# Eight instead of six of sixteen masked row block pairs merged by a VectorE copy, the two new ones in the half unit of the value products

## The chip, the core and the metric

The kernel runs on one core of a Trainium2 chip. The metric is the device time of one execution in microseconds (us), as the median of several runs. TensorE (PE in the profile; its weight loads are PEld) does the matmuls, VectorE (DVE) and ScalarE (ACT) read what it leaves in PSUM, GpSimd (POOL) works on SBUF alone, and SyncE (SP) issues nearly all DMAs.

## The reference, cut to what matters

A block with conditioning runs a sliding-window attention and then a token-mixing and a channel MLP on 2048 rows of 576. What the change touches is the attention: 32 heads of 18, and each row sees itself and the 255 rows before it.

```python
scores = jnp.einsum("bhqd,bhkd->bhqk", q, k) * (Dh ** -0.5)
idx = jnp.arange(S)
mask = (idx[:, None] - idx[None, :] >= 0) & (idx[:, None] - idx[None, :] < W)   # W = 256
scores = jnp.where(mask[None, None], scores, -1e9)
p = _softmax(scores, axis=-1)
o = jnp.einsum("bhqk,bhkd->bhqd", p, v)
```

## The kernel before, in words

The kernel has five stages: the projection to q, k and v (function `qkv`), the attention (`attention`, with the output projection and the two norms behind it, `wotile`), the token mixing (`mixing`), and the channel MLP (`mlp`). Each step is a small function, put on a list with a time by `at(t, f)`; the list is sorted by that time and run through, so the order of the instructions on each engine is written by hand. The times are an order only: each engine works through its queue in that order and waits on semaphores for what it needs.

The attention counts in half units, `n` from 0 to 31, each with the scores of two groups (`j` = 0, 1) of two heads for 512 rows; a unit `u` is two half units. Two things happen to the scores, a half unit or two apart:

- *The row maxima.* `mx(n, j, bb)` (lines 515 to 525) takes a pair of row blocks: for each of two blocks of 64 rows, one matmul (L519) gives 128 rows (two heads) by five key blocks of 64 in PSUM tile `mx`. Of the five key blocks the oldest and the newest are cut by the window's edge and by the diagonal. Where a pair isn't merged, a second matmul (L523) adds the mask `Mq` to these two blocks through the identity. `red(n, j, bb)` (lines 527 to 541) then takes the maximum of the 2 x 320 columns on VectorE (L537). In a merged pair there is no mask matmul. Where the late block is cut, the early one isn't, and the other way round, so that VectorE copies by predicate the early block over the masked places of the late one (L534) and takes the maximum of 2 x 256 columns (L535). `merged(n, j, bb)` says which of the sixteen pairs of a unit are merged (8 in each half unit: `j` 0 and 1, `bb` 0 to 3).
- *The exponentials.* Two half units and a little later `xm` computes the scores again with keys in rows (L568, and masks by L570) into two score banks `X` in turn, with the maximum folded in, and `ex` takes the exponential on ScalarE (L585).

The tiles `mx` have two buffers, by the parity of `bb`: the matmuls of a pair wait until the reduction of the pair two before has read its buffer.

In every even half unit from n = 4 on, `av(u)` gives the products of the exponentials with the values: 72 to 104 small matmuls in one go (L607), between the first pair (`mx` 0_0) and the second (0_1). Later in the same half unit their sum is copied (L612, ScalarE), turned by transposes `ot` (L617, two times four), and normalised on VectorE (`onm`: a reciprocal L624 and a product L625, each once for `r` = 0 and 1). From n = 12 to 30 the even half unit also begins one tile of the output projection: transposes `pa` and `pb` (L671, L673) into the same PSUM banks that `ot` had, copies by ScalarE (L678, L679), and the low parts by VectorE (L680, L681); its matmuls (L692) and the norm's statistics come in the odd half unit.

Of the kernel before, what the change touches and what calls it, by code (L numbers as in the profile page):

```python
# [33 lines left out]
class Kern:  # L34
# [418 lines left out]
    def attention(self, t1, t2, TA, HU, LX=2.05):  # L453
# [52 lines left out]
                nc.gpsimd.tensor_scalar(t[:, b0:, r], src[:, b0:], M[:, 2 + r:3 + r], 0.0, op0=ALU.mult, op1=ALU.add)  # L506

        def merged(n, j, bb):
            return (n >= 8 or bb >= 2) and (n % 2, j, bb) in ((0, 0, 0), (1, 0, 0), (1, 0, 1), (1, 0, 3), (1, 1, 0), (1, 1, 3))

        def mx(n, j, bb):
            g = n // 8
            pm = X["pm", n, j, bb] = ps.tile([P, 2, 512], F32, tag=f"m{bb % 2}", name=f"mx{n}_{j}_{bb}")
            Q, K = X["qs", n, j], X["K"][n % 3]
            for s in range(2):
                i = 2 * bb + s
                nb = 5 if g else min(5, i + 1)
                lhs = Q[:, i].rearrange("p r q -> p (r q)")
                nc.tensor.matmul(pm[:, s, 320 - 64 * nb:320], lhs, K[:, j, 64 * (i + 5 - nb):64 * (i + 5)], start=True, stop=merged(n, j, bb))  # L519
                if merged(n, j, bb):  # L520
                    continue
                if nb == 5:
                    nc.tensor.matmul(pm[:, s, 0:320].rearrange("p (a b) -> p a b", b=64)[:, 0::4, :], self.identr, self.Mq, start=False, stop=True)  # L523
                else:
                    nc.tensor.matmul(pm[:, s, 256:320], self.identr, self.Mq[:, 1], start=False, stop=True)

        def red(n, j, bb):
            if ("m", n) not in X:
                X["m", n] = a1([P, 16], F32, tag="m", name=f"m{n}", bufs=2)
            m, pm = X["m", n], X["pm", n, j, bb]  # L530
            c = 8 * j + 2 * bb
            if merged(n, j, bb):
                late = self.Mq[:, 1].bitcast(mybir.dt.int32).unsqueeze(1).to_broadcast([P, 2, 64])
                nc.vector.copy_predicated(pm[:, :, 256:320], late, pm[:, :, 0:64])  # L534
                nc.vector.tensor_reduce(out=m[:, c:c + 2], in_=pm[:, :, 64:320], axis=mybir.AxisListType.X, op=ALU.max, negate=True)  # L535
            elif n >= 8 or bb >= 2:
                nc.vector.tensor_reduce(out=m[:, c:c + 2], in_=pm[:, :, 0:320], axis=mybir.AxisListType.X, op=ALU.max, negate=True)  # L537
            else:
                for s in range(2):
                    w = 64 * (2 * bb + s + 1)  # L540
                    nc.vector.tensor_reduce(out=m[:, c + s:c + s + 1], in_=pm[:, s, 320 - w:320], axis=mybir.AxisListType.X, op=ALU.max, negate=True)
# [860 lines left out]
```

## Time and profile before

| | |
|---|---|
| median of 3 runs | 1775.26 us (1769.92 to 1777.12) |
| the profiled execution | 1768.65 us, span 1766.8 us |
| granted TensorE clock, mean | 0.984 |
| projections and before | up to about 211 us |
| attention, first eight half units | about 211 to 305 us |
| attention, the others | about 305 to 610 us |
| end of the attention, output projection of its last tiles | 610 to 671 us |
| token mixing and MLP | 671 to 1766.8 us |
| TensorE busy from 305 to 610 us | 298.12 of 305.00 us |
| VectorE busy from 305 to 610 us | 221.53 of 305.00 us |

The span is the time from the first to the last instruction of one execution; the device time has a little around it. An engine's busy time counts instructions that overlap once, and matmuls are pipelined: the mean duration of one is longer than the time that it adds to a queue. The chain of waits gives the latter, since it goes from start to start. In the rows, L523 is line 523 of the kernel, the number behind `x` is a count, and an arrow names what ended a wait.

### The profile page before, as it was taken

How to read it: one execution, taken by the hardware profiler on the slowest of the kernel's cores; microseconds unless marked ns; L12 is line 12 of the kernel's file. 1: busy time of each engine (PE TensorE's matmuls, PEld its weight loads, DVE VectorE, ACT ScalarE, POOL GpSimd, SP SyncE). 2: the span in 40 equal slices, each digit the busy share in tenths (PEclk: the TensorE clock that was granted, in tenths of full speed). 3: DMA queues.
4: the chain of work that ended last, by engine and by line, in shares of the span. 5: the costliest groups of instructions: out<-in, count | busy, mean ns of one | idle time of the engine just before them, and what ended most of it. 6: DMA issues, size and time to landing. Idle time of an engine off the chain costs nothing.

```text
span 1766.8 us, 33658 instructions
## 1 busy us (share of the span) xinstructions
PE 1677.2 (95%) x13369; PEld 1530.6 (87%) x13369; DVE 1106.2 (63%) x1887; ACT 704.6 (40%) x1211; POOL 898.2 (51%) x837
## 2 busy tenths in 40 slices
PE   6999998999999989987899999999899999999998
PEld 5888898899999978987688999999788999999997
DVE  6544265677777637665576666666675666666664
ACT  3222134555455454444343334433434333334331
POOL 4222357545546433555665665555635555665550
PEclk9999999999999999999899999999999999999999
DMA  8854554546556266644422112222142221112211
GB/s 259 274 178 167 169 147 131 159 133 192 151 162 172 88 189 208 208 139 154 157 63 61 47 51 63 63 64 63 59 137 60 64 63 57 44 58 63 63 45 54
DMA packets 156501, 206.79 MB, mean 117 GB/s; under 512 B 19316, under 2 KB 87924, under 8 KB 155768
## 3 DMA queue, kind: packets, MB, share of 16 engines
q1 hardware_dynamic: 155768, 203.46, 37.4%
q8 instruction: 106, 1.74, 0.4%
q10 hardware_dynamic: 576, 1.18, 0.2%
q14 instruction: 51, 0.42, 0.1%
HBM read 143.76 MB, written 60.56 MB: 116 GB/s over the span
## 4 chain that ended last, share of the span: by engine, by line
PE 80%; DVE 6%; POOL 4%; DMA 4%; issue 3%; ACT 3%; SPq 1%; POOLq 0%; DVEq 0%; ACTq 0%
PE d L1256 24%; PE qk L331 6%; PE mx L519 4%; PE X L568 4%; PE av L607 4%; PE wo L692 3%; PE v L369 3%; PE X L570 2%; PE pg L916 2%; PE w L965 1%; DVE W L1114 1%; PE ot L617 1%; DMA wmf<-in_w_mod_dram 1%; PE mx L523 1%; DMA wf<-in_B_w_dram 1%
## 5 line engine op out<-in xcount | busy, mean ns | idle before, releaser
L1256 PEld LDWEIGHTS d<-W,G 128*128 128x128 f32 x3456 | 489.4, 189 | 34.7 <-DVE acc L1264 10.1
L1256 PE MATMUL d<-W,G 128*128 128x288 f32 x3456 | 507.7, 297 | 12.2 <-DVE acc L1264 9.0
L1264 DVE TENSOR_TENSOR acc<-d,acc 128x576 f32<-128x576 f32 x288 | 216.8, 754 | 199.6 <-PE d L1256 197.5
L1094 POOL TENSOR_TENSOR wf<-wf 128x384 f32<-128x384 f32 x140 | 147.0, 1070 | 339.7 <-DMA wf<-in_B_w_dram 331.6
L585 ACT ACTIVATE P<-X 128x512 f32<-128x512 f32 (+4 forms) x320 | 178.2, 572 | 112.4 <-PE X L570 110.0
L537 DVE TENSOR_REDUCE m<-mx 128x2 f32<-128x640 f32 x144 | 117.9, 820 | 91.7 <-PE mx L523 91.1
L1233 DVE TENSOR_TENSOR G<-U,G 128x512 fp32r<-128x512 f32 x108 | 92.8, 859 | 99.4 <-ACT G L1226 99.4
L519 PE MATMUL mx<-KD,QS 128*128 128x320 f32 (+4 forms) x512 | 143.5, 340 | 11.0 <-DVE m L537 4.2
L1106 POOL TENSOR_TENSOR W<-wf,W 128x768 fp32r<-128x768 f32 x70 | 152.9, 2206 | 1.2 <-ACT W L1100 1.2
L568 PE MATMUL X<-QD,KS 128*128 128x64 f32 (+2 forms) x704 | 142.8, 295 | 3.0 <-ACT P L585 2.2
L1224 ACT ACTIVATE U<-U 128x512 f32<-128x512 f32 x108 | 68.3, 632 | 178.7 <-DVE U L1209 178.7
L499 POOL TENSOR_SCALAR QS<-QD,rowm 128x512 fp32r<-128x512 f32 x128 | 87.1, 694 | 96.3 <-DMA QD<-qd 41.5
L1224 ACT ACTIVATE C<-C 128x512 f32<-128x512 f32 x36 | 22.8, 632 | 282.5 <-DVE C L1209 282.5
L568 PEld LDWEIGHTS X<-QD,KS 128*128 128x128 f32 x704 | 106.7, 191 | 8.7 <-ACT P L585 4.8
L331 PE MATMUL qk<-hT,Wqk 128*128 128x512 f32 x462 | 109.3, 396 | 1.1 <-DVE qs L345 1.1
L506 POOL TENSOR_SCALAR KS<-KD,rowm 128x768 fp32r<-128x768 f32 (+1 forms) x128 | 108.8, 863 | 0.0
L519 PEld LDWEIGHTS mx<-KD,QS 128*128 128x128 f32 x512 | 93.1, 193 | 16.4 <-issue 7.2
L1120 POOL TENSOR_TENSOR wf<-wf,gb 128x1152 f32<-128x1152 f32 x35 | 103.1, 2945 | 7.2 <-DMA wf<-in_B_w_dram 7.2
L331 PEld LDWEIGHTS qk<-hT,Wqk 128*128 128x128 f32 x462 | 86.4, 188 | 23.4 <-DVE qs L345 1.6
L1135 POOL TENSOR_TENSOR W<-wf,W 128x1152 fp32r<-128x1152 f32 x35 | 96.7, 2763 | 6.9 <-ACT W L1129 6.9
L1100 ACT CAST W<-wf 128x1152 fp32r<-128x1152 f32 x70 | 90.4, 1320 | 20.0 <-DMA wf<-in_B_w_dram 10.5
L570 PE MATMUL X<-Mk,identr 128*128 128x256 f32 (+2 forms) x320 | 95.2, 297 | 0.0
(787 smaller groups left out, 3208.4 us busy)
## 6 DMA issues: line engine op xcount, KB each, us to landing
wf<-in_B_w_dram SPq DMA_DIRECT2D x35, 576.0 KB
wf<-in_B_w_dram SPq DMA_DIRECT2D x140, 128.0 KB
KD<-kd SPq DMA_DIRECT2D x72, 216.0 KB
QD<-qd SPq DMA_DIRECT2D x96, 144.0 KB
wf<-in_B_w_dram SPq DMA_DIRECT2D x140, 64.0 KB
qd<-qs SPq DMA_DIRECT2D x16, 512.0 KB
kd<-qs SPq DMA_DIRECT2D x16, 512.0 KB
vd<-Vst SPq DMA_DIRECT2D x16, 312.0 KB
```

The source lines that it names most:

```text
L331: nc.tensor.matmul(po, W[:, a, fs], H[:, c, :], start=(n == 0), stop=(n == 13))
L506: nc.gpsimd.tensor_scalar(t[:, b0:, r], src[:, b0:], M[:, 2 + r:3 + r], 0.0, op0=ALU.mult, op1=ALU.add)
L519: nc.tensor.matmul(pm[:, s, 320 - 64 * nb:320], lhs, K[:, j, 64 * (i + 5 - nb):64 * (i + 5)], start=True, stop=merged(n, j, bb))
L537: nc.vector.tensor_reduce(out=m[:, c:c + 2], in_=pm[:, :, 0:320], axis=mybir.AxisListType.X, op=ALU.max, negate=True)
L568: nc.tensor.matmul(px[:, c:c + q1 - q0], K[:, b + 4].rearrange("p r k -> p (r k)"), Q[:, j, q0:q1], start=(i == 0), stop=False)
L570: nc.tensor.matmul(o, self.identr, mv, start=False, stop=True)
L585: nc.scalar.activation(p[:, lo:], X["px", n, j, k][:, lo:], AF.Exp, scale=SCALE)
L1094: nc.gpsimd.tensor_tensor(out=WF[:, o], in0=WF[:, a], in1=WF[:, b], op=ALU.subtract)
L1106: eng.tensor_tensor(out=W[:, s0:s1, 3:5, :], in0=WF[:, 1 + s0:1 + s1, 0:2], in1=W[:, s0:s1, 0:2, :].bitcast(F32), op=ALU.subtract)
L1120: nc.gpsimd.tensor_tensor(out=R4, in0=R4, in1=gb.unsqueeze(1).to_broadcast([P, 2, D]), op=ALU.mult)
L1256: nc.tensor.matmul(po, G[:, g, ta, b, ts], W[:, w, b, cs], start=(n == 0), stop=(n == 5))
L1264: nc.vector.tensor_tensor(out=a, in0=po, in1=a, op=ALU.add)
```

## The change

The tuple of pairs that are merged gets two more entries, (0, 0, 1) and (0, 1, 1): the second pair of each `j` in the even half unit.

```diff
         def merged(n, j, bb):
-            return (n >= 8 or bb >= 2) and (n % 2, j, bb) in ((0, 0, 0), (1, 0, 0), (1, 0, 1), (1, 0, 3), (1, 1, 0), (1, 1, 3))
+            return (n >= 8 or bb >= 2) and (n % 2, j, bb) in ((0, 0, 0), (0, 0, 1), (0, 1, 1), (1, 0, 0), (1, 0, 1), (1, 0, 3), (1, 1, 0), (1, 1, 3))
```

On TensorE in an even half unit, just behind the value products, before (the names are those of the tiles, written and read, with their numbers):

```order
 L545 MATMUL mt_6046<-ident,m_5763 16x128
 L519 MATMUL mx_0_1_6062<-KD_1992,QS_0_5884 128x320
 L523 MATMUL mx_0_1_6062<-Mq,identr 128x2x64
 L519 MATMUL mx_0_1_6062<-KD_1992,QS_0_5884 128x320
 L523 MATMUL mx_0_1_6062<-Mq,identr 128x2x64
 L568 MATMUL X_0_1_6073<-QD_1988,KS_0_5839 128x192
```

and in the same place now:

```order
 L545 MATMUL mt_6034<-ident,m_5751 16x128
 L519 MATMUL mx_0_1_6050<-KD_1992,QS_0_5872 128x320 x2
 L568 MATMUL X_0_1_6059<-QD_1988,KS_0_5827 128x192
 L568 MATMUL X_0_1_6059<-QD_1988,KS_0_5827 128x320
 L570 MATMUL X_0_1_6059<-Mk,identr 128x2x128
```

The two mask matmuls are gone, and the score matmuls of `xm` follow the two of `mx` at once; nothing else has moved.

On VectorE in the second part of the same half unit, around the second new pair, before:

```order
 L537 TENSOR_REDUCE m_5935<-mx_1_0_6132 128x2
 L624 RECIPROCAL rc_0_6151<-ot_0_6138 128x16
 L625 TENSOR_TENSOR o_6150<-ot_0_6138,rc_0_6151 128x16x18
 L537 TENSOR_REDUCE m_5935<-mx_1_1_6154 128x2
 L624 RECIPROCAL rc_1_6174<-ot_1_6159 128x16
 L625 TENSOR_TENSOR o_6150<-ot_1_6159,rc_1_6174 128x16x18
 L537 TENSOR_REDUCE m_5935<-mx_1_2_6182 128x2
 L680 TENSOR_TENSOR T_6198<-pa_6191,T_6198 128x512
```

and now:

```order
 L537 TENSOR_REDUCE m_5923<-mx_1_0_6119 128x2
 L624 RECIPROCAL rc_0_6138<-ot_0_6125 128x16
 L625 TENSOR_TENSOR o_6137<-ot_0_6125,rc_0_6138 128x16x18
 L534 COPY_PREDICATED mx_1_1_6141<-Mq,mx_1_1_6141 128x2x64
 L535 TENSOR_REDUCE m_5923<-mx_1_1_6141 128x2
 L624 RECIPROCAL rc_1_6160<-ot_1_6144 128x16
 L625 TENSOR_TENSOR o_6137<-ot_1_6144,rc_1_6160 128x16x18
 L537 TENSOR_REDUCE m_5923<-mx_1_2_6168 128x2
 L680 TENSOR_TENSOR T_6184<-pa_6177,T_6184 128x512
```

A copy stands ahead of the reduction of pair 1_1, between the two normalisations, and that reduction is the narrow one.

## The prediction

> **What bounds the kernel now.** I read the page's first lines, then the costs by shape, then the busy time of the two kinds of half unit that alternate through the attention stage, then the waits, and last the chain of waits and the timeline of one unit. The page first:
>
> ```profile
> span 1766.8 us, 33658 instructions
> PE 1677.2 (95%) x13369; PEld 1530.6 (87%) x13369; DVE 1106.2 (63%) x1887; ACT 704.6 (40%) x1211; POOL 898.2 (51%) x837
> ```
>
> TensorE is busy for 95% of the span and VectorE for 63%, so on the whole the span is TensorE's queue. The sum below is made against this execution: 1768.65 us of device time around a span of 1766.8. It is a quick one; the runs shown have 1775.26 as their median (1769.92 to 1777.12), 6.6 us more, and I carry the difference that I work out over to that median.
>
> The costs by shape of what is removed and added (count, then busy us and mean ns of one):
>
> ```profile
> L523 PE MATMUL mx<-Mq,identr 128*128 128x128 f32 x288 | 64.6, 224 | 0.0
> L537 DVE TENSOR_REDUCE m<-mx 128x2 f32<-128x640 f32 x144 | 117.9, 820 | 91.7 <-PE mx L523 91.1
> L535 DVE TENSOR_REDUCE m<-mx 128x2 f32<-128x512 f32 x80 | 55.3, 692 | 2.8
> L534 DVE COPY_PREDICATED mx<-Mq,mx 128x128 f32<-128x128 int32 x80 | 22.9, 286 | 2.6 <-PE mx L519 2.4
> ```
>
> The 80 copies are the pairs that are merged today, and the 144 wide reductions are the pairs that still get two mask matmuls each (288). All four operations of the change are in the trace already, at the shapes that the change uses.
>
> Busy time by stretch: the first row is a half unit with value products, the second the half unit behind it.
>
> ```profile
> core 0: us, PE busy (x) PEld busy (x) DVE busy (x) ACT busy (x) POOL busy (x), PEclk, DMA share, GB/s
> 477.06:491.42 14.36, 14.21 (x282) 13.07 (x282) 10.23 (x18) 7.54 (x15) 11.39 (x17) 1.00 0.67 203
> 491.42:504.18 12.76, 12.37 (x92) 11.86 (x91) 9.60 (x22) 6.69 (x13) 2.90 (x6) 1.00 0.33 91
> ```
>
> TensorE fills 14.21 of 14.36 us where the change acts, at a granted clock of 1.00; VectorE fills 10.23. The waits of the attention stage (time, times, longest) say the same from the other side:
>
> ```profile
> DVE m L537 <- PE mx L523: 91.1, 99, 5.0
> PE mx L519 <- DVE m L537: 4.2, 12, 1.7
> ```
>
> VectorE waits 91.1 us for the mask matmul; TensorE waits only 4.2 us for a reduction, so VectorE has time to give, but not everywhere.
>
> **The change, part by part.** *How many.* A half unit n merges only where n is at least 8 or bb at least 2. The new entries are (0, 0, 1) and (0, 1, 1), both with bb = 1, so they act in the even half units n = 8 to 30: 12 halves, 24 pairs (the first four units gain none, so that eight of sixteen holds for the last twelve alone). Removed: 48 mask matmuls with their weight loads. Added: 24 copies. Turned from 640 to 512 columns: 24 reductions. No DMA, no tile and no other queue changes.
>
> *What a pair saves on TensorE.* The row of 224 ns is no price, because matmuls overlap. The chain of waits gives the time that each adds (start, us, what): an unmerged pair at the place of the first new one, and two pairs that are merged today.
>
> ```profile
> 482.66 0.15 PE mx L519
> 482.81 0.06 PE mx L523
> 482.87 0.20 PE mx L519
> 483.07 0.06 PE mx L523
> ...
> 496.88 0.29 PE mx L519 x2
> ...
> 497.47 0.41 PE mx L519 x2
> ```
>
> Unmerged 0.15 + 0.06 + 0.20 + 0.06 = 0.47 us, merged 0.29 us with score matmuls behind it: 0.18 us saved. With output-projection matmuls behind it (497.47) it takes 0.41, and 0.06 is saved. The new pairs are followed by score matmuls and by the second transposes of the value products, so I take 0.18: 24 x 0.18 = 4.3 us. The ends are 24 x 0.06 = 1.4 us, and 48 x 0.224 = 10.8 us if the whole row were time of the queue.
>
> [...]
>
> The score matmuls of a pair shrink too, from 0.15 and 0.20 to 0.29 for both; that is why a pair saves more than its two mask matmuls' 0.12.
>
> *What a pair costs on VectorE.* Its timeline over the even half unit, and a merged pair of the next one:
>
> ```profile
> 483.17 0.82 DVE L537 TENSOR_REDUCE m<-mx 128x2 f32<-128x640 f32 x1 [2.37 <-PE mx L523]
> ...
> 487.63 0.46 DVE L625 TENSOR_TENSOR o<-ot,rc 128x288 f32<-128x288 f32 x1
> 488.01 0.82 DVE L537 TENSOR_REDUCE m<-mx 128x2 f32<-128x640 f32 x1
> 488.74 0.25 DVE L624 RECIPROCAL rc<-ot 128x16 f32<-128x16 f32 x1
> 489.02 0.46 DVE L625 TENSOR_TENSOR o<-ot,rc 128x288 f32<-128x288 f32 x1
> 489.77 0.82 DVE L537 TENSOR_REDUCE m<-mx 128x2 f32<-128x640 f32 x1 [0.29 <-PE mx L523]
> 490.82 0.69 DVE L680 TENSOR_TENSOR T<-pa,T 128x512 fp32r<-128x512 f32 x1 [0.23 <-ACT T L678]
> ...
> 497.49 0.28 DVE L534 COPY_PREDICATED mx<-Mq,mx 128x128 f32<-128x128 int32 x1
> 497.81 0.69 DVE L535 TENSOR_REDUCE m<-mx 128x2 f32<-128x512 f32 x1
> 498.41 0.28 DVE L534 COPY_PREDICATED mx<-Mq,mx 128x128 f32<-128x128 int32 x1
> ```
>
> From start to start the wide reduction takes 488.74 - 488.01 = 0.73 us, copy and narrow reduction 498.41 - 497.49 = 0.92: 0.19 more for each pair. The first new pair (483.17) comes after 2.37 us of idling, so its 0.19 us costs nothing as long as the reductions behind it wait for TensorE, as most do by the 99 waits above. The second (488.01) has no idle time in front, as it stands between the two normalisations. By the first pair's saving all up to there slides 0.18 earlier, to 487.83; with 0.92 for the pair the reciprocal starts at 488.75 (before 488.74), the normalisation at 489.03, and VectorE is free at 489.49. The next reduction's matmuls are ready 0.36 earlier, at 489.41: it starts 0.08 late. That is paid from the 0.23 us of idle time in front of the projection's copy L680. So the price on the path is nothing; the cover is this 0.23, and were it gone, 12 x 0.08 = 1.0 us would be late.
>
> *Who else has to keep up.* ScalarE's exponentials set when a score bank is free:
>
> ```profile
> 483.60 0.60 ACT L585 ACTIVATE P<-X 128x512 f32<-128x512 f32 x1 [0.64 <-PE X L570]
> 487.59 0.60 ACT L585 ACTIVATE P<-X 128x512 f32<-128x512 f32 x1 [0.21 <-PE X L570]
> ```
>
> The first exponential behind the first new pair had waited 0.64 us for TensorE, and the one ahead of the second had waited 0.21: ScalarE's work starts from TensorE's and slides with it. The last stretch of the half unit leads from TensorE over ScalarE and VectorE (L680, L681, L537) back to TensorE:
>
> ```profile
> 489.73 0.45 PE pa L671 x4
> 490.18 0.02 issue
> 490.20 0.59 ACT T L678
> ...
> 492.50 0.56 PE mx L519 x2
> ```
>
> It begins with a TensorE transpose (489.73) that comes 0.36 earlier, so its end, the matmul that waits for the last reduction at 492.50, comes 0.36 earlier too.
>
> *The sum.* 12 half units x 2 pairs x (0.18 on TensorE + 0 on VectorE) = 4.3 us, which nothing behind the stage gives back, as the stages that follow start from its last matmul. 1768.65 - 4.3 = 1764.4 for an execution like the profiled one; 1775.26 - 4.3 = 1771.0 for the median, 0.24% less. By over 0.5% (8.9 us) is about what a measurement of this kernel can tell from no change, so I forecast no difference that can be told.
>
> **Rivals.**
>
> *The whole busy time goes.* If the queue shortened by 0.224 us for each removed matmul, 10.8 us, the median would be 1764.5, 0.6% faster. For it: TensorE is the bound and its weight loads go as well. Against it: the chain gives these matmuls 0.06 us each, and a pair 0.18.
>
> *VectorE becomes the bound: slower than before.* The place is the transpose pb, which writes the bank that the second normalisation reads:
>
> ```profile
> 490.00 0.27 PE L673 MATMUL pb<-ident,or 128*128 128x128 f32 x1
> ```
>
> It would come at 489.64, and VectorE has finished at 489.49. If VectorE is over 0.15 us later than I work out, TensorE's whole queue stands there, the saving is eaten, and at worst the extra 0.19 of each of the 24 pairs comes on top: 4.6 us, 1779.9. For it: there is no idle time between 487.63 and 489.02. Against it: 0.29 and 0.23 of idle time follow. To be slower by over 0.5% each of the 12 units would have to lose 0.74 us, more than a whole wide reduction holds VectorE (0.73).
>
> [...]
>
> *Only the first pair counts.* If the three-engine stretch from 489.73 to 492.50 is held by VectorE or ScalarE, the second saving is idle time: 12 x 0.18 = 2.2 us, 1773.1. For it: TensorE does wait there. Against it: the stretch starts from TensorE.
>
> **How the numbers follow.** The forecast has 0.72, only the first pair 0.13, the whole busy time 0.07, VectorE the bound 0.08. With the runs spread over 7.2 us, about 0.05 of the forecast's chance comes out over 0.5% faster, so faster is 0.07 + 0.05 = 0.12; half of VectorE's case is put beyond 0.5%, so slower is 0.04; the same is left 0.84. The range goes from 1764.5 less 1.5 to 1779.9, the ends of the unknown costs: 1763 to 1780. The likeliest case alone, with its ends of 1.4 and 4.3 and half the spread, is 1767 to 1777.
>
> **What would show it.** Mask matmuls L523 240 in place of 288, L537 120, L534 and L535 104 each. In the chain, the pair behind the value products at about 0.29 in place of 0.47. A half unit with value products of 14.0 in place of 14.36 us, the other unchanged at 12.76, and the reduction at 489.77 without idle time in front of it. A row "PE pb" that waits for VectorE, or a wait of TensorE for a reduction much over 4.2 us in sum, would show the VectorE rival, and a unit that is shorter by 0.18 that only the first pair counts. The forecast is wrong if the half units shorten and the end of the program does not.

## The result and the profile after

The changed kernel takes 1762.08 us (median of 4 runs, 1759.46 to 1764.23), the kernel before beside it 1775.9 (1769.92 to 1777.12): a ratio of 0.9946, 95% interval 0.992 to 0.9973, so 9.6 us less, with 4.8 to 14.2 possible. (The two medians, of four runs each, lie 13.8 us apart; that is near the far end of the interval.) Two repeats on other occasions gave 0.9947 (0.9925 to 0.9968) and 0.9949 (0.9926 to 0.9973). The forecast was 0.9976. The gain is real and about twice the 4.3 us of the sum; the question is where the other half is from.

The profiled execution after took 1759.46 us. Its page, and the groups by shape that the change touches:

```profile
span 1757.6 us, 33586 instructions
...
PE 1668.2 (95%) x13321; PEld 1522.8 (87%) x13321; DVE 1108.8 (63%) x1911; ACT 704.3 (40%) x1211; POOL 898.9 (51%) x837
```

```profile
L537 DVE TENSOR_REDUCE m<-mx 128x2 f32<-128x640 f32 x120 | 98.0, 819 | 51.0 <-PE mx L523 50.5
...
L535 DVE TENSOR_REDUCE m<-mx 128x2 f32<-128x512 f32 x104 | 71.9, 691 | 3.6
...
L523 PE MATMUL mx<-Mq,identr 128*128 128x128 f32 x240 | 53.5, 223 | 0.0
...
L534 DVE COPY_PREDICATED mx<-Mq,mx 128x128 f32<-128x128 int32 x104 | 29.9, 287 | 36.6 <-PE mx L519 36.5
```

The counts are those forecast: 48 matmuls and 48 weight loads fewer, 24 copies more. VectorE's 91.1 us of waiting for the mask matmul has become 50.5 + 36.5 us, the latter in front of the copy, which now waits for the score matmul. The waits of the attention stage and the two half units that the prediction showed:

```profile
DVE m L537 <- PE mx L523: 50.5, 75, 2.1
...
DVE mx L534 <- PE mx L519: 36.5, 17, 6.1
...
PE mx L519 <- DVE m L537: 4.0, 12, 1.6
```

```profile
473.40:487.10 13.70, 13.70 (x278) 12.93 (x278) 10.45 (x20) 7.53 (x15) 10.73 (x17) 1.00 0.69 205
487.10:499.87 12.77, 12.39 (x92) 11.89 (x92) 9.61 (x22) 6.70 (x13) 3.55 (x6) 1.00 0.38 100
```

TensorE waits for a reduction as little as before (4.0 us, before 4.2). The half unit with value products went from 14.36 to 13.70 us, the other stayed (12.76, now 12.77). In the chain of waits of that half unit (start, us, what) both new pairs are short, and the stretch over ScalarE and VectorE at its end is what it was:

```profile
478.54 0.21 PE mt L545
478.74 0.29 PE mx L519 x2
...
483.35 0.30 PE mx L519 x2
...
485.42 0.45 PE pa L671 x4
...
488.19 0.57 PE mx L519 x2
```

VectorE's timeline there:

```profile
479.07 0.29 DVE L534 COPY_PREDICATED mx<-Mq,mx 128x128 f32<-128x128 int32 x1 [1.94 <-PE mx L519]
...
483.87 0.28 DVE L534 COPY_PREDICATED mx<-Mq,mx 128x128 f32<-128x128 int32 x1
484.19 0.69 DVE L535 TENSOR_REDUCE m<-mx 128x2 f32<-128x512 f32 x1
484.80 0.25 DVE L624 RECIPROCAL rc<-ot 128x16 f32<-128x16 f32 x1
485.08 0.46 DVE L625 TENSOR_TENSOR o<-ot,rc 128x288 f32<-128x288 f32 x1
485.45 0.82 DVE L537 TENSOR_REDUCE m<-mx 128x2 f32<-128x640 f32 x1
486.51 0.69 DVE L680 TENSOR_TENSOR T<-pa,T 128x512 fp32r<-128x512 f32 x1 [0.23 <-ACT T L678]
```

The first new copy has 1.94 us of idle time ahead of it, the second none, and the reduction at 485.45 starts without idle time and not late: it stands 0.03 us behind the transpose `pa` (485.42), before 0.04 (489.77 and 489.73).

To see where the 9.1 us between the two profiled executions lie, I took the starts of the same TensorE instruction in both (us; *av* is the first value product L607, *mt* L545, *wo* the run of L692 of a group):

```
                                                     before   after   difference
start to the first av                                252.34  249.31     -3.03
first to sixth av (three changed half units)         116.52  117.65     +1.13
sixth av to the last half unit (nine changed)        247.27  242.75     -4.52
last half unit to the last av                         14.19   15.60     +1.41
last av to the first wo behind it (the 21st group)    13.71   10.56     -3.15
21st to 23rd wo                                        9.68    6.90     -2.78
from there to the end                               1113.08 1114.88     +1.80
```

The first row can't be the change, since up to there both kernels issue the same instructions; it is the granted clock (a window of before, then of after, from 220 to 230 us, the clock third from the right):

```profile
220.00:230.00 10.00, 8.83 (x40) 8.05 (x41) 6.25 (x16) 0.25 (x1) 6.06 (x10) 0.67 0.59 170
```

```profile
220.00:230.00 10.00, 9.17 (x60) 8.00 (x60) 8.03 (x21) 0.25 (x1) 6.33 (x10) 1.00 0.72 225
```

The +1.41, -2.78 and +1.80 have such stretches at half clock in them too (3.4 us from 613.6 on and from 794.5 on in after only, 6.8 us from 643.2 on in before only). The second row, whose three changed half units should give -1.1, holds the value products, whose time varies from unit to unit (from 4.74 to 6.21 us, below). What is left is the stage and the 3.15 us from the first of the last value products to the output projection, which no term of the sum names. Of the stage's 4.52, the value products, whose time varies, hold 1.2; the parts of the half units that the pairs are in hold the other 3.3 (nine half units). The timelines there, TensorE's rows and then the first of ScalarE's weight copies L849; before:

```profile
630.32 4.31 PE L607 MATMUL av<-P,V 64*32 64x320 f32 x163
637.38 0.91 PE L607 MATMUL av<-P,V 64*32 64x192 f32 x45 [2.75 <-issue]
...
644.04 3.73 PE L692 MATMUL wo<-Wo,T 128*128 128x288 f32 x14 [3.96 <-DVE T L680]
...
638.06 0.62 ACT L849 CAST W<-w1r 128x512 fp32r<-128x512 f32 x1 [7.04 <-PE av L607]
```

and after:

```profile
625.31 4.84 PE L607 MATMUL av<-P,V 64*32 64x320 f32 x208
630.09 0.55 PE L671 MATMUL pa<-ident,or 128*128 128x128 f32 x3
631.90 0.33 PE L671 MATMUL pa<-ident,or 128*128 128x128 f32 x1 [1.27 <-issue]
...
635.88 2.12 PE L692 MATMUL wo<-Wo,T 128*128 128x288 f32 x14 [2.44 <-DVE T L680]
...
629.91 0.62 ACT L849 CAST W<-w1r 128x512 fp32r<-128x512 f32 x1 [3.89 <-DMA xmt<-xnd]
```

In both, TensorE stops once with nothing that the profile names ("issue"). Before, 45 value products are left at the stop (of 208 in the trace, where each of the program's 104 matmuls of a unit is two); after, it comes three transposes behind the last of them. 45 + 3 is 48, the number of matmuls that the change took out: counted along TensorE's queue, matmuls and weight loads together, it is the same place, about instruction 13,285. And it matters on which side of ScalarE's copies it lies. These wait for one of the last value products: in both traces the wait ends 0.03 us behind the semaphore of one with about 30 left (637.99 and 629.84 us), though the row of after names a DMA that landed about then. Behind them stand VectorE's weight splits, its copies L680 and L681, and the matmul L692: from the first copy to L692 it takes 644.04 - 638.06 = 5.98 us before and 635.88 - 629.91 = 5.97 after. A stop ahead of their release delayed all of it here (13.71 us in the table, from the first of the last value products to the first *wo*); the one behind it passed while ScalarE and VectorE worked (10.56 us).

### The profile page after: what moved, and what is told of

Read it like the earlier page. It is cut to its first block, busy times and chain, and to the rows that moved or that the text cites. A ratio compares the mean times of both kernels' runs of the same rounds, so it can differ in the third digit from the quotient of the medians.

```text
span 1757.6 us, 33586 instructions
## 1 busy us (share of the span) xinstructions
PE 1668.2 (95%) x13321; PEld 1522.8 (87%) x13321; DVE 1108.8 (63%) x1911; ACT 704.3 (40%) x1211; POOL 898.9 (51%) x837
## 4 chain that ended last, share of the span: by engine, by line
PE 79%; DVE 6%; POOL 4%; DMA 4%; issue 3%; ACT 3%; SPq 1%; POOLq 0%; DVEq 0%; ACTq 0%
PE d L1256 24%; PE qk L331 6%; PE mx L519 4%; PE X L568 4%; PE av L607 4%; PE wo L692 3%; PE v L369 3%; PE pg L916 2%; PE X L570 2%; DVE W L1114 1%; PE w L965 1%; PE ot L617 1%; DMA wmf<-in_w_mod_dram 1%; PE mx L523 1%; PE u13P L1203 1%
## 5 line engine op out<-in xcount | busy, mean ns | idle before, releaser
L519 PE MATMUL mx<-KD,QS 128*128 128x320 f32 (+4 forms) x512 | 139.2, 335 | 12.3 <-DVE m L537 4.0
L568 PE MATMUL X<-QD,KS 128*128 128x64 f32 (+2 forms) x704 | 143.0, 296 | 3.3 <-ACT P L585 2.1
L537 DVE TENSOR_REDUCE m<-mx 128x2 f32<-128x640 f32 x120 | 98.0, 819 | 51.0 <-PE mx L523 50.5
L568 PEld LDWEIGHTS X<-QD,KS 128*128 128x128 f32 x704 | 107.8, 192 | 9.4 <-ACT P L585 6.1
L570 PE MATMUL X<-Mk,identr 128*128 128x256 f32 (+2 forms) x320 | 95.6, 299 | 0.2 <-issue 0.2
```

The costliest lines, as they stand in the source:

```text
L568: nc.tensor.matmul(px[:, c:c + q1 - q0], K[:, b + 4].rearrange("p r k -> p (r k)"), Q[:, j, q0:q1], start=(i == 0), stop=False)
L570: nc.tensor.matmul(o, self.identr, mv, start=False, stop=True)
```

## The experiments

The theory: what the sum missed is this stop, at a fixed place of the instruction stream, which any 48 matmuls fewer ahead of it would move past the release; the pairs themselves are worth what the sum says. The rivals: the rest is scatter of the clock, as in the first row of the table; or the pairs are worth more than the chain says; or only one of them counts. "Left" below is the number of value products (of 208) still to do at the stop: 45, less the matmuls taken out ahead of it, plus those put in.

### The two kernels again

No edit. `before_again`:

> The kernel before once more, unchanged, for a second profile. Theory A (a stop of TensorE's queue at a fixed place in its stream of instructions): TensorE stops for about 2.7 us, waiting for nothing that the profile names, at its 13285th matmul or weight load, inside the last value products (unit 15), as in the first profile, and the stretch from the last transpose of maxima (L545, number 31) to the first output-projection matmul of the tail (L692, number 22) takes 37 to 38 us (first profile 37.6). Theory C (chance, by the clock or by a DMA): no stop there, or one of another length and place, and a stretch nearer to the 33.1 us of the changed kernel. Time in both: the same as before within 0.3%.

`after_again`:

> The changed kernel once more, for a second profile and a tighter ratio. Theory A: the stop stands at the same number of TensorE's stream (13284 in the first profile), which is now behind the last value products, between the transposes pa; the stretch from L545 number 31 to L692 number 22 takes about 33 us; ratio to before 0.993 to 0.996. Theory C: the stretch scatters between 33 and 38 us and the ratio comes back to about 0.9975, the 4.3 us of the sum.

`after_third`:

> The changed kernel again, on the same chip as the two beside it, to tighten its ratio and for a third profile: 0.9947, rest of the even half unit 10.50 us, stretch from the last value products to the output projection 10.5 us.

Measured: 0.9992 (0.9971 to 1.0013), and the two ratios of the changed kernel above. The stop repeats to the instruction: in before_again with 45 left, 2.19 us long,

```profile
636.90 0.91 PE L607 MATMUL av<-P,V 64*32 64x192 f32 x45 [2.19 <-issue]
...
643.55 3.73 PE L692 MATMUL wo<-Wo,T 128*128 128x288 f32 x14 [3.95 <-DVE T L680]
```

and in both repeats of the changed kernel behind three transposes `pa` (1.55 and 2.37 us). From the last *av* to the 21st *wo* it took 13.15 us in before_again, 10.56 and 10.56 in the two others. So this part isn't scatter. The clock's part is not settled by it: the stretch at half clock at 223 us came back in before_again and stayed away in both repeats of after.

### One pair alone

```diff
-in ((0, 0, 0), (0, 0, 1), (0, 1, 1), (1, 0, 0), ...)
+in ((0, 0, 0), (0, 0, 1), (1, 0, 0), ...)        # first_only, first_again
+in ((0, 0, 0), (0, 1, 1), (1, 0, 0), ...)        # second_only
```

`first_only`:

> Only the first new entry, (0, 0, 1): 24 mask matmuls and their weight loads less, 12 pairs merged. Theory A: 12 x 0.18 to 0.2 = 2.2 to 2.4 us less, and no more, since 48 instructions fewer leave the stop at number 13284 still inside the last value products (numbers 12910 to 13325): ratio about 0.9987, the stop of 2.7 us still there. Rival B (a pair itself is worth more than the chain of waits says): half of the whole gain, ratio about 0.997. Rival of the prediction, only the first pair counts: ratio as with both.

`second_only`:

> Only the second new entry, (0, 1, 1). Theory A: 2.2 to 2.4 us less, ratio about 0.9987, the stop of 2.7 us still inside the last value products; the even half unit shorter by 0.18 us. Rival B: ratio about 0.997. Rival of the prediction, only the first pair counts: no gain, the half unit unchanged at 14.36 us, or slower where VectorE becomes the bound.

`first_again`:

> Only the first new entry, once more, as its ratio of 0.9943 (0.9922 to 0.9965) was as large as with both. By the stretches of the profiles it should be 12 x 0.22 = 2.7 us in the even half units and about 3.7 us in the tail, 6.4 us: ratio 0.9964. If the second entry is worth nothing in time, whatever the stretches say: 0.9943 again.

Measured: 0.9943 (0.9922 to 0.9965) for the first pair alone, and 0.9962 (0.9944 to 0.998) when it ran again; 0.997 (0.9948 to 0.9991) for the second alone. What an even half unit takes from its L545 to the next (median of nine in the steady stage, *av* not included) is 10.88 us before, 10.66 with the first pair, 10.72 with the second, 10.50 with both: 0.22 + 0.16 = 0.38, so both count and they add up. The expectation on the end was wrong. The stop stayed where it was expected, 24 matmuls nearer to the end of the value products, but it cost nothing there (first_only, TensorE; ScalarE's first copy; then second_only):

```profile
636.76 0.52 PE L607 MATMUL av<-P,V 64*32 64x128 f32 x21 [1.18 <-issue]
...
641.42 2.79 PE L692 MATMUL wo<-Wo,T 128*128 128x288 f32 x14 [2.35 <-DVE T L680]
...
635.50 0.62 ACT L849 CAST W<-w1r 128x512 fp32r<-128x512 f32 x1 [3.89 <-DMA xmt<-xnd]
```

```profile
635.81 0.52 PE L607 MATMUL av<-P,V 64*32 64x128 f32 x21 [1.73 <-issue]
...
639.92 2.12 PE L692 MATMUL wo<-Wo,T 128*128 128x288 f32 x14 [1.80 <-DVE T L680]
```

With 21 left, ScalarE's copies begin at 635.50, ahead of the stop (635.59 to 636.76), and the stretch takes 10.52 us in both kernels. I had taken the end of the value products for the border; it is the release of ScalarE's copies, somewhere between 45 and 21 left. The single pairs therefore have the whole gain of the end, and only about half that of the stage.

### The change with the place put back

48 tiny matmuls at the start of the program, far from everything, as many as the change removes (the pads write a PSUM tile that nothing reads):

```diff
+    def pad(self, n):
+        po = self.ps.tile([P, 6, 64], F32, tag="s2", name="pad")
+        for i in range(n):
+            self.nc.tensor.matmul(po[0:32, 0, :], self.identr[:, 0:32], self.zero, start=True, stop=True)
...
+        at(-61, self.pad, 48)                     # after_pad24: 24
```

`after_pad`, the changed kernel with 48:

> The changed kernel with 48 tiny matmuls (32 by 64) at the start of TensorE's queue, where it idles for its first 8 us: 96 weight loads and matmuls more, as many as the change removed, so that the last value products have the same numbers in the stream as before the change (12958 to 13373). Theory A (a stop at a fixed number of the stream, on the path only where it comes ahead of the matmul that releases ScalarE's weight copies): the stop at 13285 is back inside the last value products, the stretch from their first matmul to the output projection's (L607 number 16 to L692 number 21) goes from 10.5 back to 13.1 to 13.7 us, the even half units stay short (0.37 us each), and the ratio to before comes to about 0.9975. Rival (the tail's gain comes from the merged pairs themselves, or from their earlier end): 10.5 us, ratio 0.9945.

`before_pad`, the kernel before with 48:

> The kernel before with the same 48 tiny matmuls: the price of the padding itself. Both theories: ratio within 0.2% of 1, the stretch of the last value products to the output projection 13 us or more (theory A: the stop at 13285 now comes 96 places earlier in the last value products, still ahead of the release).

`after_pad24`, the changed kernel with 24:

> The changed kernel with 24 tiny matmuls at the start, half the padding: 48 instructions, so that the stop of TensorE's queue (number 13285) falls where it fell with one new pair alone, about 40 places before the end of the last value products, behind the release of ScalarE's copies. Theory A: the stop is inside the last value products, the stretch to the output projection is 10.5 us all the same, ratio about 0.9947, against 0.9981 with twice the padding. Rival (each instruction of padding costs, wherever it puts the stop): half way, stretch 11.5 us, ratio 0.9964.

Measured: after_pad 0.9981 (0.9964 to 0.9998), before_pad 0.9996 (0.9975 to 1.0016), after_pad24 0.9945 (0.9924 to 0.9965). The rows (after_pad, before_pad, after_pad24; lines are 6 higher, L607 is L613):

```profile
634.68 0.91 PE L613 MATMUL av<-P,V 64*32 64x192 f32 x45 [1.65 <-issue]
...
641.33 3.73 PE L698 MATMUL wo<-Wo,T 128*128 128x288 f32 x14 [3.95 <-DVE T L686]
...
635.36 0.62 ACT L855 CAST W<-w1r 128x512 fp32r<-128x512 f32 x1 [5.94 <-PE av L613]
```

```profile
630.93 2.52 PE L613 MATMUL av<-P,V 64*32 64x320 f32 x93 [0.48 <-issue]
...
639.19 3.44 PE L698 MATMUL wo<-Wo,T 128*128 128x288 f32 x14 [3.54 <-DVE T L686]
```

```profile
629.87 0.52 PE L613 MATMUL av<-P,V 64*32 64x128 f32 x21 [1.46 <-issue]
...
634.24 2.12 PE L698 MATMUL wo<-Wo,T 128*128 128x288 f32 x14 [2.05 <-DVE T L686]
```

This is the experiment that decides. Left are 45, 93 and 21, exactly as the count demands. With the 48 put back, the changed kernel has its stop at 45 left again and ScalarE's copies wait for it (5.94 us, "PE av"): the stretch is 12.61 us in place of 10.56, its half units stay at 10.50, and of the gain 3.4 us are left (0.3 to 6.4), which fits the 4.3 of the sum. With 24 of the 48 the stop is behind the release, the stretch is 10.51, and the whole gain is there. In time alone this is close: the interval of after_pad (from 0.9964) just meets those of the three runs without pads (up to 0.9973), so that the decision rests on the stop and the stretch in the profiles. What 48 pads cost by themselves wasn't measured apart, but up to the first *av* they cost nothing that shows (251.97 and 251.77 us, before 252.34 and 251.64), and 24 cost nothing in all. In before_pad the stop was short (0.48) and the stretch fell to 11.66, yet the time did not fall; 2 us is within that run's interval.

### Other pairs

```diff
+in ((0, 0, 0), (1, 0, 0), (1, 0, 1), (1, 0, 2), (1, 0, 3), ...)              # odd_one: before and (1, 0, 2)
+in ((0, 0, 0), (0, 0, 1), (0, 0, 2), (0, 1, 1), (1, 0, 0), ...)              # nine: after and (0, 0, 2)
+            return n >= 8 or bb >= 2                                          # all16
```

`odd_one`, the kernel before with one pair more in the half unit that has no value products:

> The kernel before with one more pair merged in the odd half unit instead, (1, 0, 2): 16 pairs (12 units, and the first four too, as bb is 2), 32 mask matmuls less. Theory A: 16 x 0.18 = 2.9 us less in the odd half units, none in the even ones, and the tail's 13.4 us become 10.5, since 64 instructions fewer also put the release ahead of the stop: together about 6 us, ratio about 0.9965. Rival (the tail's gain belongs to the even half units' pairs): 2.9 us alone, ratio 0.9984, tail 13.4 us.

`nine`, the changed kernel with a ninth pair:

> The changed kernel with one more pair of the even half unit merged, (0, 0, 2): 12 pairs, 24 mask matmuls less. If VectorE still has time behind the value products (it idled 0.56, 0.18 and 0.23 us ahead of the three reductions behind the first new pair): the rest of the even half unit goes from 10.50 to about 10.33 us, 2.0 us in all, and the ratio to before to about 0.9935. If VectorE is used up there, as it was in the odd half unit with one pair more (10.90 to 10.93 us): 10.50 or above, ratio 0.9947 or worse.

`all16`, every pair:

> All sixteen pairs of a unit merged (from n = 8 on, and those with bb 2 and 3 before): 288 fewer mask matmuls than before, 144 copies more. If each pair is worth 0.18 us: 26 us less, ratio 0.985. If VectorE becomes the bound, as the rival of the prediction has it: TensorE waits for reductions for far more than 9 us in sum, the three-engine stretch from pa to the next reduction grows by 0.2 us or more, and the gain stays under half of that, ratio 0.992 or above.

Measured: odd_one 0.9979 (0.9961 to 0.9997), nine 0.9967 (0.9947 to 0.9986), all16 1.0003 (0.9986 to 1.0021).

odd_one removes 32 matmuls and its half units gain nothing: the odd ones take 10.93 us (10.90 before), the even ones stay, where I had expected 2.9 us in all. VectorE runs without idle time between its pairs there,

```profile
496.22 0.45 DVE L696 TENSOR_TENSOR xr<-wo,xr 128x288 f32<-128x288 f32 x1
496.59 0.28 DVE L534 COPY_PREDICATED mx<-Mq,mx 128x128 f32<-128x128 int32 x1
496.90 0.69 DVE L535 TENSOR_REDUCE m<-mx 128x2 f32<-128x512 f32 x1
497.51 0.28 DVE L534 COPY_PREDICATED mx<-Mq,mx 128x128 f32<-128x128 int32 x1
```

so there is no idle time left that could pay for the new copy. The trace shows where the saving goes. Behind L545 of the half unit at 465.80 us TensorE reaches the mask matmul L570 after the new pair at 3.75 us, where the kernel before takes 3.98; then it idles 0.24 us for the buffer of the new pair, which VectorE has read at 3.96 (before 3.94). It is faster by 3.7 us (0.5 to 6.9) all the same, and its end shows why: 45 - 32 = 13 left, a stretch of 10.51 us.

```profile
638.29 0.34 PE L607 MATMUL av<-P,V 64*32 64x64 f32 x13 [1.70 <-issue]
...
642.37 2.11 PE L692 MATMUL wo<-Wo,T 128*128 128x288 f32 x14 [1.96 <-DVE T L680]
```

This is the end's gain without the stage's; after_pad is the stage's without the end's. Together they are 3.4 + 3.7 = 7.1 us, and the change gave 9.6 (4.8 to 14.2).

nine adds 32 removals that don't pay: its even half unit takes 10.49 us (10.33 expected), 10.50 without them. Here it isn't VectorE that takes the saving, since it still idles 0.28 us in front of a reduction two pairs on (481.46 us). TensorE comes only 0.05 us earlier to the end of the pair behind the ninth (2.63 in place of 2.69 us behind L545, medians), and the score matmuls after it start at 2.88 in both kernels. What they wait for is ScalarE's exponentials, which free the score banks: from 340 to 600 us TensorE's weight loads L568 wait 19 times for them, 3.5 us in sum, where the changed kernel has 5 times and 0.8. At its end the count gives 45 - 80 = -35 left. But the places where TensorE stops in these profiles lie multiples of 128 of these matmuls apart, 256 instructions with their weight loads (shown in the last part). The one before is at -35 + 128 = 93 left, as in before_pad, and there TensorE does stop, for 0.21 us. The stretch is 11.39 us, near before_pad's 11.66:

```profile
625.57 2.52 PE L607 MATMUL av<-P,V 64*32 64x320 f32 x93 [0.21 <-issue]
...
633.83 3.73 PE L692 MATMUL wo<-Wo,T 128*128 128x288 f32 x14 [3.12 <-DVE T L680]
```

all16 shows VectorE's rival come true, only further on: even half units at 10.63 and odd ones at 11.28, 0.38 over before, and TensorE waits 10.5 us in the stage for the narrow reduction (1.4 before):

```profile
PE mx L519 <- DVE m L535: 10.5, 18, 2.4
```

Its end has a stop ahead of the release again, and a stretch of 12.81 us:

```profile
641.14 0.89 PE L607 MATMUL av<-P,V 64*32 64x192 f32 x43 [1.76 <-issue]
```

No kernel here is clearly ahead of the changed one.

## Why the prediction came out as it did

By the ratio the time is 0.9946 x 1775.26 = 1765.7 us, inside the range and 5.3 under the forecast; the median of the first four runs, 1762.08, is 0.9 under its low end. "Within 0.5%" had 0.84 and the change is just beyond it.

- *What a pair saves on TensorE: right.* 0.47 us became 0.29 and 0.30. Both pairs together give 0.38 in a half unit where 0.36 was worked out, 12 x 0.38 = 4.6 us where the sum has 4.3. The row of 224 ns would have given 0.90 a half unit, so the rival of the whole busy time is out, though the time itself looks like its 10.8 us: a total that fits is no evidence for its mechanism.
- *The half unit of 14.0: half right.* It fell to 13.70, but 0.25 of the 0.3 beyond the forecast is the value products' (477.06 to 482.45 before, 473.40 to 478.54 after), whose stops for "issue" vary in length: their stretch takes from 4.74 to 6.21 us over the nine steady units of the fourteen profiles. The forecast should have been given for the part behind L545.
- *VectorE at nothing: right, and with more room than worked out.* The reduction was to start 0.08 late and didn't, since from the normalisation to it are 0.37 us (485.08 to 485.45) and not the row's 0.46, and the 0.23 in front of L680 is whole. How little more it has was not forecast: in the odd half unit the next pair's saving went into a wait for it (odd_one), while in the even one the next pair's went into a wait for ScalarE (nine).
- *ScalarE and the three-engine stretch slide along: right.* 488.19 - 485.42 = 2.77 us, and 492.50 - 489.73 = 2.77 before.
- *Only the first pair counts: out.* The second alone gives 0.16.
- *"Which nothing behind the stage gives back, as the stages that follow start from its last matmul": the step that failed.* Nothing gave it back, but the step took for granted that what follows stays as it was. Removing 96 instructions moved a stop in TensorE's queue from ahead of the release of ScalarE's copies to behind it. The missing term is 13.71 - 10.56 = 3.15 us in the first pair of profiles and 13.15 - 10.56 = 2.59 in the second; with it the sum is 7.2 to 7.7 us (4.6 for the pairs as measured), which the interval of the result holds. That the number came out inside the range is in part luck: the stage's term was right, and the missing one happened to be small enough. The row was there to be read: 2.75 us of "issue" within the last value products, the longest such wait of TensorE's matmuls in the attention stage and its end, and no buffer, engine or DMA to account for it.

The other 2 us of the result are within its interval, and the granted clock of the single runs says more. An estimate: in a straight-line fit over the 254 runs whose clock is on record, a run takes 1.24 us less than another of its own kernel for each 0.001 that its mean granted clock is higher (95% interval 1.07 to 1.41). Brought to one clock in this way, after_again and after_third are on the mean 7.6 us (6.1 to 9.0) ahead of the kernel before beside them, which is what the two terms give; after_pad is 5.2 ahead, odd_one 1.7 and before_pad 1.4, each give or take 2. What the ratios have above that is in part a clock that was higher in the changed kernel's runs (0.9844 and 0.9845 on the mean, against 0.9838 and 0.9841), for a reason that isn't shown, and in part scatter.

## What to carry to other kernels

Before costing an edit that removes or adds instructions, look for long waits of the bounding engine with the releaser "issue" and ask what hangs on the instructions right behind them: such a stop can belong to a place in the instruction stream (here the stops lay multiples of 256 instructions of the engine apart, semaphore waits counted), and the edit then moves it against the program. To part an edit's own worth from this, run it with as many empty instructions added early as it removes; if half the gain goes with them, that half was luck of placement (a pad alone that puts the stop behind the release was not run). And merging was paid for here by idle time of VectorE near the pair, in front of it or soon behind (the second new pair had none in front, but 0.29 and 0.23 us behind). What TensorE saved lasted only to its next wait: in odd_one that was for VectorE (0.24 us), in nine for ScalarE (19 times, 3.5 us in sum).

## What the runs showed of the hardware

*Stops 256 instructions apart.* In twelve of the fourteen profiles the stop stands where the count of removed and added matmuls puts it (93, 45, 21 or 13 left, or three transposes behind), 0.48 to 2.75 us long, and it goes with the count when a pad is put in hundreds of microseconds earlier. The other two, nine and all16, show the spacing. Numbered from 0 along TensorE's queue, with the waits for semaphores counted too, the stop is at 13,505 in the twelve; in nine it is at 13,249, which is 256 less, and in all16 at 12,993, which is 512 less (all16 has 60 more semaphore waits in its queue, so that matmuls alone don't give its 43 left). The stops in the middle of the stage belong to the same row: from 326 us on, all 67 places of the fourteen profiles where one instruction of the value products starts over 0.3 us behind the one before it lie at a number that leaves 193 when divided by 256. Not every such place has a stop. Why the length varies stays open.

*Packets of instructions.* The trace has a DMA queue whose kind is "instruction" (before: packets, MB, share of 16 engines):

```profile
q8 instruction: 106, 1.74, 0.4%
```

1.74 MB in 106 packets are 16.4 KB each. TensorE's queue has 27,102 instructions in that trace, weight loads and semaphore waits counted: if all 106 packets are TensorE's, an estimate from the two is 256 instructions to a packet (after: 27,006 and 105, 257). In all fourteen profiles the last packet ahead of the end of the stop starts 2.29 to 2.75 us before TensorE resumes (before: 634.94 and 637.38), whatever the length of the stop. Where TensorE passes such a place within the value products without a stop (from 300 us on), the last packet started at least 2.27 us earlier, mostly over 4. That would fit a wait for a packet, but no run shows one: in none were the packets changed and the program not. So the cause of the stop is open, while its place and its price are measured: up to 2.75 us, within 208 small matmuls and as many weight loads that take 4.84 us when nothing stops them (after, 625.31).

*Half clock.* Stretches of 3.4, 6.8 or more us at a granted clock of 0.5 come at places many of which differ from profile to profile. The one at 223 us (6.8 us long in before) was there in before and before_again, both runs of the first pair alone, nine, all16 and both kernels with 48 pads, and absent in all three of after, after_pad24, second_only and odd_one, though in before, before_again, both runs of the first pair, all three of after and second_only TensorE's instructions up to there are the same. It costs about 3 us in the profile (252.34 us up to the first *av* in before, 249.31 in after), and the kernels' times don't follow this one stretch (first_only had it, at a ratio of 0.9943, and second_only not, at 0.997), though the time of a run follows its mean clock by the estimate above (1.24 us for each 0.001). Why the stretches come where they do is open.
